# Two turns without dense products, gate steps and second product inside a mixture unit, chunk loads two units ahead

## The chip, the cores and the metric

The kernel runs on one core of one Trainium2 chip. The metric is the device time of one execution in microseconds. Three runs of the kernel before gave 909.3, 910.09 and 910.9, median 910.09 us.

## The reference

Three layers follow each other. The first is a landmark (Nyström) attention over 4 batches x 8 heads x 576 positions x 64 features; the second a dense softplus layer; the third a mixture of 8 experts of which each token uses one.

```python
k_lm = k.reshape(B, H, 32, 18, D).mean(axis=3)      # q_lm likewise
A, Bm, C = sm(q, k_lm), sm(q_lm, k_lm), sm(q_lm, k) # softmax of scaled scores
for _ in range(6):
    Z = 2 * Z - Z @ Bm @ Z                          # Newton steps to an inverse
x = A @ Z @ C @ v                                   # -> [2304, 512]
h = x @ w_in                                        # [2304, 2048]
g = np.maximum(h, 0.0) + np.log1p(np.exp(-np.abs(h)))
x = g @ w_out                                       # [2304, 512]
e_idx = argmax(x @ w_gate)                          # one of 8 experts a token
out = gate_w * sigmoid(x @ w_ogate)[e_idx] * (relu(x @ w1[e_idx]) @ w2[e_idx])
```

The weights of the dense layer arrive as 64-bit floats and are decoded on the chip.

## The kernel before

**Attention stage.** Steps named in a string (PLAN) are called one after the other: K and V load a group of four heads, T turns its keys and queries (`transposes`, line 178), M makes landmarks, A and C score, N inverts, E and F multiply out; X, W and O prepare the first chunk and the first weights. There are eight groups, g = 0 to 7. This part of the program is not written in its final order: a planner with costs for the instructions places them on the engines, so that the groups are interleaved. In a turn each of the 2 x 4 head tiles takes a PSUM bank (two of them, tag `pt`), puts a dense 128x512 product of ones into it (`warm`, line 159, whose result is overwritten), three transposes, and an eviction by ScalarE (line 187).

**Dense stage.** It stands under a manual schedule: each engine runs its instructions in the order of the code. The 2304 tokens are nine chunks c of 256; a pair p is two of the sixteen blocks of 128 columns of `w_in`. A mixture unit i (loop of line 882) is one (c, p) of the list `order`, 72 in all. It consists of

- the first product `gemm1` (line 628): 24 matmuls, twelve for each column block, from a high and a low part of tokens and weights (three products for one), into one of two PSUM banks of tag `h`;
- `softplus` (line 641): four ScalarE instructions (t, t, u, l), three of VectorE (u, d, l), then gh on ScalarE and gl on VectorE, the two parts of the result. The tiles t, u, l, d have one buffer, gh and gl three;
- the second product `gemm2` of unit i - 2 (LAG = 2): 12 matmuls into the chunk's accumulators.

The bank of `gemm1` is free again when d has read it, so unit i + 2 waits for d of unit i. The first 24 units (nj = 24) mix chunks 0, 1 and 2, with one pair of chunk 0 ahead; from unit 24 on the chunks follow one another, eight units each.

**Weights within the first 24 units.** Blocks 8 to 15 of `w_in` and 3 to 15 of `w_out` are decoded meanwhile by a generator (`weights`, line 573) of 64 weight steps: one to begin, then three for each of 21 jobs (high part on ScalarE with the start of the next job; low part on VectorE; three VectorE instructions that end the next job's decode). `softplus` calls three weight steps in each unit from 1 on: after its first ScalarE part, after gh, after gl. EXTRA = 0, 5, 8 adds one after unit 0 and three each after units 5 and 8. The jobs are sorted by the unit that needs them; blocks 12 and 13 of `w_in` are jobs 13 and 14 and are read first by unit 16 (chunk 0, pair 6), blocks 14 and 15 are jobs 17 and 18 and are read first by unit 19.

**Chunk loads.** The tokens of chunk 3 are loaded at the head of unit 23 and split after its softplus; those of chunk c + 1 are loaded and split (`load_xr`, `split_x`, lines 604 and 620) in one place, after the softplus of unit (c, 5). The loads are issued by SP's queue, which also stores the gated chunks (line 751) in the order of the code. The two load buffers carry the tag `deca` that the weight jobs use too.

**Gate steps.** When a chunk's second product is complete, `gate` (line 676) copies it out of PSUM (two ScalarE copies of line 679), and then continues in steps: transposes of one half with their ScalarE copy (line 690), logits of that half (line 695), the same for the other half, the choice of the expert on VectorE, ranks (a small matmul), and reciprocal and store. A list of waiting steps, `side`, is taken up one step after `gemm1` and one at the end of a unit; in the units 65 to 72 (`fast`) also one in the middle of each product, by `hook`. The part `early`, which finds the most frequent expert, follows the gate of chunk 7 in that list.

**Expert stage.** 23 slots of 128 gathered tokens, each with the weights of one expert, loaded and split while the slot before is multiplied. The change does not touch it.

Of the kernel before, what the change touches and what calls it, by code (L numbers as in the profile page):

```python
# [41 lines left out]
"""  # L42
NWA = 8
NWO = 3
EXTRA = 0, 5, 8
JOINT = 3
NFIRST = 2
TAIL = 0, 2, 1, 0, 1, 1, 0, 0, 1, 0, 1, 0, 0, 0, 1, 1
# [62 lines left out]
def chain(*gens):  # L111
    for g_ in gens:
        yield from g_
# [3 lines left out]
def moe_nystrom_kernel(ctx: ExitStack, tc: tile.TileContext, q, k, v, w_in, w_out, w_gate, w_ogate, w1, w2,  # L117
# [26 lines left out]
    with ExitStack() as actx:  # L144
# [14 lines left out]
        def warm(ps):  # L159

            nc.tensor.matmul(ps, dense[:, :128], dense, start=True, stop=True)  # L161
# [16 lines left out]
        def transposes(r, g):  # L178
            for nm in ("k", "q"):
                xt = a2.tile([128, 4, HALF], F32, tag=nm + "T", name=nm + "T", bufs=3)  # L180
                for h in range(4):
                    ps = pt.tile([128, 512], F32, tag="pt", name="ps_t")
                    warm(ps)
                    for c in range(3):
                        nc.tensor.transpose(ps[:, c * TP:(c + 1) * TP], r[nm][:, h, c * 128:(c + 1) * 128],  # L185
                                            ident[:TP, :TP])
                    nc.scalar.activation(xt[:, h], ps[:, :HALF], AF.Copy)
                    yield
                r[nm + "T"] = xt
# [355 lines left out]
    with ExitStack() as mctx:  # L545
# [58 lines left out]
        def load_xr(c):  # L604
            if c <= JOINT - 1:
                t = m2.tile([128, 4, CH], F32, tag="x2", name="xr", bufs=3)
                xr = [t[:, :2], t[:, 2:]]
            else:
                xr = [m2.tile([128, 2, CH], F32, tag="deca", name="xr") for _ in range(2)]
            t0 = c * CH  # L610
            while t0 < (c + 1) * CH:
                b, o = divmod(t0, S)
                n = min(S - o, (c + 1) * CH - t0)
                for j in range(2):
                    nc.sync.dma_start(xr[j][:, :, t0 - c * CH:t0 - c * CH + n],
                                      xT_d[b].rearrange("(k p) n -> p k n", p=128)[:, 2 * j:2 * j + 2, o:o + n])
                t0 += n
            return xr
# [19 lines left out]
                    hook()  # L638
            return ps

        def softplus(h, units):

            t = sp.tile([128, 2, CH], F32, tag="t", name="t")
            u = sp.tile([128, 2, CH], F32, tag="u", name="u")
            l = sp.tile([128, 2, CH], F32, tag="l", name="l")
            d = sp.tile([128, 2, CH], F32, tag="d", name="d")
            gh = m3.tile([128, 2, CH], F32R, tag="gh", name="gh")
            gl = m3.tile([128, 2, CH], F32R, tag="gl", name="gl")
            nc.scalar.activation(t, h, AF.Abs)
            nc.scalar.activation(t, t, AF.Exp, scale=-1.0)  # L650
            nc.scalar.activation(u, t, AF.Identity, bias=1.0)  # L651
            nc.scalar.activation(l, t, AF.Ln, bias=1.0)
            units(1)
            nc.vector.scalar_tensor_tensor(u, u, -1.0, t, ALU.add, ALU.subtract)  # L654
            nc.vector.scalar_tensor_tensor(d, h, 0.0, u, ALU.max, ALU.subtract)  # L655
            nc.vector.tensor_tensor(l, l, d, ALU.add)  # L656
            nc.scalar.activation(gh, l, AF.Copy)  # L657
            units(1)
            nc.vector.tensor_tensor(gl, l, gh.bitcast(F32), ALU.subtract)  # L659
            units(1)  # L660
            return gh, gl

        def gemm2(p, g, acc):
            for i in range(2):
# [188 lines left out]
        with tc.manual_schedule():  # L853
# [19 lines left out]
            def units(n):  # L873
                for _ in range(n):
                    next(work, None)
# [6 lines left out]
            for i in range(len(order) + LAG):  # L882
                fast[0] = len(order) - np_ <= i - LAG + 1 < len(order)
                if i == len(order):
                    for _ in side:
                        pass
                    win_ctx.close()
                    rw = ctx.enter_context(tc.tile_pool(name="rw", bufs=1, side="right", reuse_waits="tile"))
                    for j in range(4):
                        raw.append(rw.tile([128, 4, 512], F32, name=f"raw{j}"))  # L890
                    for _ in range(2):
                        ring[0].append([rw.tile([128, 4, 512], F32R, name=f"{n}{len(ring[0]) + 4}") for n in ("hi", "lo")])
                    wk[0] = splits(0, NBASE)
                if i < len(order):
                    c, p = order[i]
                    if i == nj - 1:
                        xr.append(load_xr(JOINT))
                    h = gemm1(p, xs[c], *HB.get(i, ()))
                    if i > nj + LAG:
                        next(side, None)  # L900
                    gs[i] = softplus(h, units if i else int)
                    if i in EXTRA:
                        units(1 if i == 0 else 3)
                    if i == 2:
                        nc.vector.tensor_copy(tri_b, cc("tri"))
                        nc.vector.tensor_copy(one_b, cc("ones"))
                        nc.vector.memset(osum[:, 0], 0.0)
                        nc.vector.tensor_copy(sgn[:, 0], cc("iota")[:1, :NE])
                        nc.vector.tensor_scalar(sgn[:, 1], cc("iota")[:1, :NE], -1.0, None, ALU.mult)
                        for nm, src in ((0, w_gate), (1, w_ogate)):  # L910
                            nc.sync.dma_start(wg[:, :, nm * NE:(nm + 1) * NE], src.rearrange("(k p) e -> p k e", p=128))
                    if i == nj - 1:
                        xs[JOINT] = split_x(xr.pop(0))
                    if p == 5 and JOINT - 1 < c < NCH - 1:
                        xs[c + 1] = split_x(load_xr(c + 1))
                if i >= len(order):
                    xt[i - len(order)] = t_x(i - len(order))
                    wunits(2)
                if i >= LAG:
                    c2, p2 = order[i - LAG]  # L920
                    if p2 == 0:
                        tags = first[c2] if c2 < JOINT else first[c2 % 2]
                        accs[c2] = [(pa if "acc" in t else pb).tile([128, 512], F32, tag=t, name=t) for t in tags]
                    gemm2(p2, gs.pop(i - LAG), accs[c2])
                    if p2 == np_ - 1:
                        ga_ = gate(c2, accs.pop(c2))
                        next(ga_)
                        side = chain(side, ga_)
                        if c2 == NCH - 2:
                            side = chain(side, early())  # L930
                if nj + LAG < i < len(order) + LAG - 1:
                    next(side, None)
            side = chain(side, route())


# [154 lines left out]
```

## Time and profile before

| | us |
|---|---|
| median of three runs | 910.09 |
| the profiled execution, as a run | 910.2 |
| its span from the first to the last instruction | 908.4 |
| around the span | 1.8 |
| TensorE busy | 859.9 (95% of the span) |
| VectorE busy | 666.5 (73%) |
| ScalarE busy | 586.9 (65%) |
| GpSimd busy | 209.5 (23%) |
| mean granted TensorE clock | 0.988 |

The attention stage takes the span up to about 136 us (its last products run till 152), the dense stage from there to about 594, the expert stage the rest. A busy share of TensorE comes from matmuls whose ends are modelled and overlap; what counts below is when each begins. A row of the timeline reads: start, duration, engine, line, operation, out<-in, shape, number merged; in brackets the idle time of the engine before it and what ended that. PE is TensorE, DVE is VectorE, ACT is ScalarE, SPq is the issuing of transfers by SyncE.

### The profile page before, as it was taken

The page shows a single profiled execution, that of the slowest core. Times are in us where ns is not written, and L with a number is a line of the kernel's source. Part 1 is how long each engine was busy: PE and PEld are TensorE (multiplying, and loading weights), DVE is VectorE, ACT ScalarE, POOL GpSimd, SP SyncE. Part 2 cuts the span into 40 slices and gives each one's busy share as a digit, 9 for nine tenths or more (in the row PEclk, how much of TensorE's full clock was granted, in tenths as well). Part 3 has the DMA queues.
Part 4 walks back from the last instruction along what each step waited for, and adds up shares of the span by engine and source line. Part 5 has one row for each costly group of instructions (what it writes and reads, how often), then busy time and mean ns, then how long its engine had stood idle before and what let it go on. Part 6 is the DMA issues. An engine that isn't in the chain of part 4 may idle for free.

```text
span 908.4 us, 15419 instructions
## 1 busy us (share of the span) xinstructions
PE 859.9 (95%) x5826; PEld 718.9 (79%) x5826; DVE 666.5 (73%) x1121; ACT 586.9 (65%) x958; POOL 209.5 (23%) x109
## 2 busy tenths in 40 slices
PE   6998987989998999998999998989999999999996
PEld 3665655888997999998899997877888888888885
DVE  0856697999984465556556463668799999999994
ACT  2554565767774655555455554465888888888883
POOL 0001131000000000000000000034666667666662
PEclk9999999999999999999999999999999999999998
DMA  9856555333300000101011000141118369521600
GB/s 222 196 140 183 158 189 166 95 116 97 113 24 24 1 25 1 47 24 47 1 48 47 1 25 1 47 186 59 36 40 292 148 222 366 185 105 35 232 26 33
DMA packets 49516, 90.92 MB, mean 100 GB/s; under 512 B 5471, under 2 KB 32095, under 8 KB 47392
## 3 DMA queue, kind: packets, MB, share of 16 engines
q1 hardware_dynamic: 41408, 74.43, 26.6%
q0 software_dynamic: 3680, 10.78, 3.7%
q10 hardware_dynamic: 4352, 4.72, 1.5%
q8 instruction: 46, 0.75, 0.4%
q14 instruction: 30, 0.25, 0.1%
HBM read 134.46 MB, written 15.48 MB: 165 GB/s over the span
## 4 chain that ended last, share of the span: by engine, by line
PE 68%; DVE 14%; DMA 6%; ACT 6%; issue 4%; POOL 0%; SPq 0%; DVEq 0%; POOLq 0%; ACTq 0%
PE ps_h L635 19%; PE acc L670 15%; PE ps_g L960 10%; PE ps_y L985 9%; DMA raw<-in_moe_w 3%; DVE lo L479 2%; DVE dect L101 2%; PE ps_hT L974 2%; ACT hi L477 2%; PE ps_lg L695 2%; DVE deca L102 1%; PE ps_t L185 1%; PE ps_t L161 1%; DVE l L656 1%; DVE d L655 1%
## 5 line engine op out<-in xcount | busy, mean ns | idle before, releaser
L479 DVE TENSOR_TENSOR lo<-raw,hi 128x1024 fp32r<-128x1024 f32 x129 | 226.3, 1781 | 11.4 <-ACT hi L477 11.1
L477 ACT ACTIVATE hi<-raw 128x1024 fp32r<-128x1024 f32 x176 | 176.9, 1063 | 8.5 <-DMA raw<-in_moe_w 8.1
L635 PE MATMUL ps_h<-xh,whi 128*128 128x256 f32 x512 | 148.1, 289 | 7.7 <-DVE d L655 4.8
L635 PE MATMUL ps_h<-xl,whi 128*128 128x256 f32 x512 | 146.3, 286 | 0.4 <-DVE xl L108 0.4
L635 PE MATMUL ps_h<-xh,wlo 128*128 128x256 f32 x512 | 146.2, 286 | 0.0
L486 POOL DMA_INDIRECT xg<-x_d,gidx x23 | 37.0, 1610 | 444.1 <-ACT t L650 433.1
L479 POOL TENSOR_TENSOR lo<-raw,hi 128x1024 fp32r<-128x1024 f32 x47 | 116.7, 2485 | 35.8 <-ACT hi L477 35.6
L657 ACT ACTIVATE gh<-l 128x512 fp32r<-128x512 f32 x72 | 45.5, 632 | 116.0 <-DVE l L656 116.0
L654 DVE SCALAR_TENSOR_TENSOR u<-u,t 128x512 f32<-128x512 f32 x72 | 49.6, 688 | 83.5 <-ACT u L651 83.4
L635 PEld LDWEIGHTS ps_h<-xh,whi 128*128 128x128 f32 x512 | 99.2, 194 | 13.6 <-DVE d L655 6.1
L670 PE MATMUL acc<-woh,gh 128*128 128x512 f32 x256 | 103.1, 403 | 1.6 <-ACT gh L657 1.6
L670 PE MATMUL acc<-wol,gh 128*128 128x512 f32 x256 | 101.0, 394 | 0.0
L635 PEld LDWEIGHTS ps_h<-xl,whi 128*128 128x128 f32 x512 | 99.2, 194 | 2.2 <-DVE xl L108 0.6
L670 PE MATMUL acc<-woh,gl 128*128 128x512 f32 x256 | 100.8, 394 | 0.0
L635 PEld LDWEIGHTS ps_h<-xh,wlo 128*128 128x128 f32 x512 | 99.4, 194 | 0.0
L659 DVE TENSOR_TENSOR gl<-l,gh 128x512 fp32r<-128x512 f32 x72 | 49.9, 693 | 38.8 <-ACT gh L657 37.0
L985 PE MATMUL ps_y<-hi,woh 128*128 128x512 f32 x184 | 76.7, 417 | 0.2 <-ACT woh L977 0.2
L985 PE MATMUL ps_y<-hi,wol 128*128 128x512 f32 x184 | 73.3, 398 | 1.4 <-DVE wol L978 1.3
L960 PE MATMUL ps_g<-hi,x0l 128*128 128x512 f32 x184 | 73.9, 402 | 0.3
L985 PE MATMUL ps_y<-lo,woh 128*128 128x512 f32 x184 | 72.7, 395 | 0.0
L960 PE MATMUL ps_g<-hi,x0h 128*128 128x512 f32 x184 | 72.1, 392 | 0.0
L960 PE MATMUL ps_g<-lo,x0h 128*128 128x512 f32 x184 | 71.9, 391 | 0.0
(246 smaller groups left out, 1756.6 us busy)
## 6 DMA issues: line engine op xcount, KB each, us to landing
raw<-in_moe_w SPq DMA_DIRECT2D x88, 1024.0 KB
raw<-in_moe_w_in SPq DMA_DIRECT2D x16, 512.0 KB
raw<-in_moe_w_out SPq DMA_DIRECT2D x16, 512.0 KB
x_d<-x SPq DMA_DIRECT2D x9, 514.0 KB
k<-in_k SPq DMA_DIRECT2D x8, 576.0 KB
q<-in_q SPq DMA_DIRECT2D x8, 576.0 KB
v<-in_v SPq DMA_DIRECT2D x8, 576.0 KB
xT_d<-xo ACTq DMA_DIRECT2D x16, 288.0 KB
```

The lines of the kernel that those rows point to most:

```text
L101: nc.vector.scalar_tensor_tensor(t, hi32, -0x80000000, t, ALU.bitwise_and, ALU.bitwise_or)
L477: nc.scalar.activation(w[0][:, us], raw[i][:, us], AF.Copy)
L479: eng.tensor_tensor(w[1][:, us], raw[i][:, us], w[0][:, us].bitcast(F32), ALU.subtract)
L486: nc.gpsimd.indirect_dma_start(out=xg, out_offset=None, in_=src, in_offset=bass.IndirectOffsetOnAxis(ap=gidx[:, s:s + 1], axis=0))
L635: nc.tensor.matmul(ps[:, i], a[:, kk], b_[:, kk], start=n == 0, stop=n == 11)
L654: nc.vector.scalar_tensor_tensor(u, u, -1.0, t, ALU.add, ALU.subtract)
L657: nc.scalar.activation(gh, l, AF.Copy)
L659: nc.vector.tensor_tensor(gl, l, gh.bitcast(F32), ALU.subtract)
L670: nc.tensor.matmul(acc[tt], a[:, i, ts_], b_[f], start=f == 0 and n == 0, stop=f == NFF - 1 and n == 2)
L695: nc.tensor.matmul(pl[:, :2 * NE], xt[tt][:, kk], wg[:, kk], start=kk == 0, stop=kk == 3)
L960: nc.tensor.matmul(ps, a[:, kk], b_[:, kk], start=n == 0, stop=n == 11)
L985: nc.tensor.matmul(y, a[:, kk], b_[:, kk], start=half == 0 and n == 0, stop=half == 1 and n == 11)
```

## The change

- The turns of groups 3 and 4 lose their dense products, eight each.
- `softplus` becomes a generator of four parts. Its first two parts (the ScalarE four, the VectorE three) stay behind `gemm1`; then come `gemm2` of unit i - 2 with the gate steps at its middle and end and the copies that begin a gate; then gh, and then gl. In ScalarE's and VectorE's queues the end-of-unit gate step now stands ahead of gh and gl. TensorE's order is not altered.
- EXTRA = 15, 15, 15: after unit 15 three weight steps more; none after 0, 5 and 8 (unit 0 has its one step by the new rule).
- The load of chunk 3 stands at the end of unit 21 and its split at the end of unit 22; the load of chunk c + 1 at the end of unit (c, 3), its split at the end of unit (c, 5).

```diff
--- before.py
+++ after.py
@@ -42,7 +42,7 @@
 """
 NWA = 8
 NWO = 3
-EXTRA = 0, 5, 8
+EXTRA = 15, 15, 15
 JOINT = 3
 NFIRST = 2
 TAIL = 0, 2, 1, 0, 1, 1, 0, 0, 1, 0, 1, 0, 0, 0, 1, 1
@@ -180,7 +180,8 @@
                 xt = a2.tile([128, 4, HALF], F32, tag=nm + "T", name=nm + "T", bufs=3)
                 for h in range(4):
                     ps = pt.tile([128, 512], F32, tag="pt", name="ps_t")
-                    warm(ps)
+                    if g not in (3, 4):
+                        warm(ps)
                     for c in range(3):
                         nc.tensor.transpose(ps[:, c * TP:(c + 1) * TP], r[nm][:, h, c * 128:(c + 1) * 128],
                                             ident[:TP, :TP])
@@ -638,27 +639,27 @@
                     hook()
             return ps
 
-        def softplus(h, units):
+        def softplus(h):
 
             t = sp.tile([128, 2, CH], F32, tag="t", name="t")
             u = sp.tile([128, 2, CH], F32, tag="u", name="u")
             l = sp.tile([128, 2, CH], F32, tag="l", name="l")
             d = sp.tile([128, 2, CH], F32, tag="d", name="d")
-            gh = m3.tile([128, 2, CH], F32R, tag="gh", name="gh")
-            gl = m3.tile([128, 2, CH], F32R, tag="gl", name="gl")
             nc.scalar.activation(t, h, AF.Abs)
             nc.scalar.activation(t, t, AF.Exp, scale=-1.0)
             nc.scalar.activation(u, t, AF.Identity, bias=1.0)
             nc.scalar.activation(l, t, AF.Ln, bias=1.0)
-            units(1)
+            yield
             nc.vector.scalar_tensor_tensor(u, u, -1.0, t, ALU.add, ALU.subtract)
             nc.vector.scalar_tensor_tensor(d, h, 0.0, u, ALU.max, ALU.subtract)
             nc.vector.tensor_tensor(l, l, d, ALU.add)
+            yield
+            gh = m3.tile([128, 2, CH], F32R, tag="gh", name="gh")
+            gl = m3.tile([128, 2, CH], F32R, tag="gl", name="gl")
             nc.scalar.activation(gh, l, AF.Copy)
-            units(1)
+            yield
             nc.vector.tensor_tensor(gl, l, gh.bitcast(F32), ALU.subtract)
-            units(1)
-            return gh, gl
+            yield gh, gl
 
         def gemm2(p, g, acc):
             for i in range(2):
@@ -893,26 +894,13 @@
                     wk[0] = splits(0, NBASE)
                 if i < len(order):
                     c, p = order[i]
-                    if i == nj - 1:
-                        xr.append(load_xr(JOINT))
-                    h = gemm1(p, xs[c], *HB.get(i, ()))
+                    g = softplus(gemm1(p, xs[c], *HB.get(i, ())))
                     if i > nj + LAG:
                         next(side, None)
-                    gs[i] = softplus(h, units if i else int)
-                    if i in EXTRA:
-                        units(1 if i == 0 else 3)
-                    if i == 2:
-                        nc.vector.tensor_copy(tri_b, cc("tri"))
-                        nc.vector.tensor_copy(one_b, cc("ones"))
-                        nc.vector.memset(osum[:, 0], 0.0)
-                        nc.vector.tensor_copy(sgn[:, 0], cc("iota")[:1, :NE])
-                        nc.vector.tensor_scalar(sgn[:, 1], cc("iota")[:1, :NE], -1.0, None, ALU.mult)
-                        for nm, src in ((0, w_gate), (1, w_ogate)):
-                            nc.sync.dma_start(wg[:, :, nm * NE:(nm + 1) * NE], src.rearrange("(k p) e -> p k e", p=128))
-                    if i == nj - 1:
-                        xs[JOINT] = split_x(xr.pop(0))
-                    if p == 5 and JOINT - 1 < c < NCH - 1:
-                        xs[c + 1] = split_x(load_xr(c + 1))
+                    next(g)
+                    if 0 < i < nj:
+                        units(1)
+                    next(g)
                 if i >= len(order):
                     xt[i - len(order)] = t_x(i - len(order))
                     wunits(2)
@@ -930,6 +918,25 @@
                             side = chain(side, early())
                 if nj + LAG < i < len(order) + LAG - 1:
                     next(side, None)
+                if i < len(order):
+                    next(g)
+                    if 0 < i < nj:
+                        units(1)
+                    gs[i] = next(g)
+                    if i < nj:
+                        units(1 + EXTRA.count(i))
+                    if i == 2:
+                        nc.vector.tensor_copy(tri_b, cc("tri"))
+                        nc.vector.tensor_copy(one_b, cc("ones"))
+                        nc.vector.memset(osum[:, 0], 0.0)
+                        nc.vector.tensor_copy(sgn[:, 0], cc("iota")[:1, :NE])
+                        nc.vector.tensor_scalar(sgn[:, 1], cc("iota")[:1, :NE], -1.0, None, ALU.mult)
+                        for nm, src in ((0, w_gate), (1, w_ogate)):
+                            nc.sync.dma_start(wg[:, :, nm * NE:(nm + 1) * NE], src.rearrange("(k p) e -> p k e", p=128))
+                    if i == nj - 3 or p == 3 and JOINT - 1 < c < NCH - 1:
+                        xr.append(load_xr(max(c + 1, JOINT)))
+                    if i == nj - 2 or p == 5 and JOINT - 1 < c < NCH - 1:
+                        xs[max(c + 1, JOINT)] = split_x(xr.pop(0))
             side = chain(side, route())
```

## Rows read from the trace of the kernel before

**Rows 1.** The page's chain that ended last, shares of the span by engine

```profile
PE 68%; DVE 14%; DMA 6%; ACT 6%; issue 4%; POOL 0%; SPq 0%; DVEq 0%; POOLq 0%; ACTq 0%
```

**Rows 2.** Chain that ended last, in order of time: start, us, what

```profile
13.45 0.48 PE ps_t L185 x3
...
287.53 4.34 PE ps_h L635 x23
...
300.44 2.87 PE ps_h L635 x24
303.31 2.75 PE acc L670 x12
...
431.07 4.31 PE acc L670 x12
...
561.67 4.47 PE ps_h L635 x24
```

**Rows 3.** Waits of PE, 160 to 600: waiter, releaser, us in total, times, longest

```profile
PE ps_h L635 <- DVE d L655: 4.8, 3, 2.4
...
PE ps_h L635 <- ACT xh L107: 2.8, 1, 2.8
PE ps_n L767 <- DVE cd L736: 1.8, 1, 1.8
PE ps_tr L689 <- ACT x L679: 1.8, 2, 1.4
```

**Rows 4.** Timeline, ACT at the turn to chunk 3

```profile
286.06 1.13 ACT L107 ACTIVATE xh<-xr 128x512 fp32r<-128x512 f32 x2
```

**Rows 5.** Windows: length, busy us (count) by engine, clock, DMA share, GB/s

```profile
288.00:292.00 4.00, 4.00 (x23) 4.00 (x22) 0.08 (x1) 0.03 (x1) 0.00 (x0) 0.59 0.50 131
...
560.00:564.00 4.00, 3.39 (x21) 3.39 (x22) 2.06 (x9) 0.55 (x2) 0.00 (x0) 0.73 0.00 0
```

**Rows 6.** Timeline, the load and split of chunk 6

```profile
422.91 0.36 SPq L751 DMA_DIRECT2D x_d<-x  x1
...
423.36 2.44 SPq L615 DMA_DIRECT2D xr<-xT_d  x4
...
428.32 1.15 ACT L107 ACTIVATE xh<-xr 128x512 fp32r<-128x512 f32 x2 [1.60 <-DMA xr<-xT_d]
...
430.01 1.07 PE L695 MATMUL ps_lg<-wg,x2t 128*128 128x16 f32 x8 [2.51 <-ACT x2t L690]
```

**Rows 7.** Timeline, gate of chunk 7

```profile
559.98 0.58 ACT L690 ACTIVATE x2t<-ps_tr 128x512 f32<-128x512 f32 x1
...
560.61 1.06 PE L695 MATMUL ps_lg<-wg,x2t 128*128 128x16 f32 x8 [1.36 <-ACT x2t L690]
```

**Rows 8.** Timeline, first 24 units: PE's waits for d, VectorE's unit

```profile
177.34 0.39 PE L635 MATMUL ps_h<-xh,whi 128*128 128x256 f32 x1 [0.24 <-DVE d L655]
...
210.57 0.39 PE L635 MATMUL ps_h<-xh,whi 128*128 128x256 f32 x1 [2.17 <-DVE d L655]
...
242.06 0.69 DVE L655 SCALAR_TENSOR_TENSOR d<-ps_h,u 128x512 f32<-128x512 f32 x1
...
243.47 0.69 DVE L599 TENSOR_TENSOR wol<-deca,woh 128x512 fp32r<-128x512 f32 x1
...
247.44 0.69 DVE L655 SCALAR_TENSOR_TENSOR d<-ps_h,u 128x512 f32<-128x512 f32 x1
```

**Rows 9.** Timeline, the turn of group 3 and the first piece of group 5's

```profile
46.54 0.39 PE L161 MATMUL ps_t<-dense 128*128 128x512 bf16 x1
46.77 0.41 PE L185 MATMUL ps_t<-cst,k 96*128 96x96 f32 x3
...
47.21 0.90 ACT L187 ACTIVATE kT<-ps_t 128x288 f32<-128x288 f32 x2 [0.23 <-PE ps_t L185]
...
48.34 0.90 ACT L187 ACTIVATE kT<-ps_t 128x288 f32<-128x288 f32 x2 [0.23 <-PE ps_t L185]
...
73.52 0.39 PE L161 MATMUL ps_t<-dense 128*128 128x512 bf16 x1
```

## The prediction

> **What bounds the kernel.** I read the page's chain of work first: TensorE holds 68% of it [rows 1], so a microsecond counts where TensorE stands still or runs slowly. The chain in order of time then shows the dense stage at its best: a first product in 2.87 us and a second in 2.75, one after the other, 5.62 us a unit [rows 2]. TensorE can't be shortened there except by its interruptions, and the table of TensorE's waits lists them, each a handful of places rather than a pattern [rows 3]. The chain has a second sign of an interruption: pieces that take 4.3 to 4.5 us where 2.75 to 2.87 are usual [rows 2]. They follow the waits, and the granted clock falls in them (0.59 in the mean of 288 to 292, 0.73 in 560 to 564 [rows 5]; 1.00 is the 2.4 GHz level, so part of such a stretch runs at 1.2). So a wait of 1.4 to 2.8 us costs up to 1.6 us more behind it, though not each does.
>
> **Loads in front, chunk 3.** Now the split stands behind the softplus of unit 23, and ScalarE gets to xh at 286.06 [rows 4], when TensorE has waited for most of 2.8 us [rows 3]; it runs freely only from 287.53, 0.9 us behind xh's first half (286.06 + about 0.57), because xl comes later. Then 23 matmuls take 4.34 us instead of 2.75. Together 2.8 + 0.9 + 1.6 = 5.3. After the change the split ends unit 22, one unit (5.62 us) earlier. xh and xl then take some 2.5 us behind gl of unit 22, and unit 24 begins about 4 us behind that point, so nothing is late: **-5.2**. The split pushes the softplus of unit 23 back by its 1.13 us of ScalarE; the two banks give d far more room than that. The load needs the buffers that the last weight job gives back in unit 20, and is issued in unit 21, so it has landed when unit 22 ends.
>
> **Loads in front, chunk 6.** SP stores chunk 3's gate result at 422.91 and only then issues the four loads, at 423.36; ScalarE reaches the split and stands 1.60 us for the data; the gate's copy is queued behind that, and TensorE waits 2.51 us for it before its logits [rows 6]. The second product behind it takes 4.31 instead of 2.75 us [rows 2]. At pair 3 the load is ahead of that store in SP's queue, two units earlier: -2.5 - 1.6 = **-4.1**. The other turns show no wait and gain nothing. What is queued behind the earlier loads on SP are only stores that nobody waits for in that stretch.
>
> **Gate steps ahead of gh.** ScalarE idles between l's first part and gh, because VectorE's three instructions come between. A copy or exponential that fits there is free. Before, the copies that begin a gate and the copy of the second turn stood behind gh; in chunk 7's gate TensorE waited 1.4 us for the first, 1.36 for the second (ScalarE starts it at 559.98, TensorE runs on at 560.61) and 1.8 for VectorE to free the bank of the ranks [rows 3, 7]; another 0.4 of the same kind lies at chunk 4's gate (1.8 in two waits, the longest 1.4 [rows 3]). The first product after the second wait took 4.47 instead of 2.87 [rows 2]. With gh behind them, both copies are done before TensorE asks. The ranks' bank depends on VectorE's work behind l of unit 67, which starts earlier by gl and its wait (about 1.2 us), so some 0.6 of 1.8 remain; and `early`, whose VectorE work is not shortened, now comes last: I expect 0.7 of a new wait at its second matmul. Sum: 1.4 + 1.4 + 1.8 + 1.6 - 0.6 - 0.7 + 0.4 = 5.3, **-5.3**. gl itself comes later by the gate's VectorE work (at most some 2.5 us in a unit), but unit i + 2 uses it, 11 us later. Moving `gemm2` into the unit alters no order on TensorE: nothing.
>
> **EXTRA.** The two long waits for d are the price of the extra steps after units 5 and 8: 2.4 and 2.17 [rows 3, 8]. They go, -4.6. But the weights come later. Unit 16 reads block 13, whose low part is weight step 45. Before, steps 1 + 3 x 12 + 6 = 43 are done after unit 12, and 45 falls into unit 13. Now 1 + 3 x 14 = 43 are done after unit 14, and 45 is the middle step of unit 15: its VectorE instruction stands behind d and l of unit 15, and ends 1.4 us after d (243.47 + 0.69 against 242.06 + 0.69 [rows 8]). How early is d? VectorE needs 5.38 us a unit (242.06 to 247.44) and TensorE 5.62, so d gains 0.24 a unit from where it was just in time, the 0.24 us wait at 177.34 for unit 6 [rows 8]: by unit 15's d eleven units, 2.6 us ahead of unit 17's start. The low part is then ready 1.2 us ahead of unit 17. Unit 16 wants it in its second half, 1.6 us after its own start, so 4.0 us ahead of unit 17. TensorE waits about 2.8 there, inside a first product. Unit 19 meets the same with block 15 (step 57, the middle of unit 18), because the three extra steps after unit 15 take VectorE back by about what the wait gave: some 2.4. Gains 4.6, new waits about 5: **+0.3**. Bounds: -4.6 if no weight is late, +3.5 if both waits are followed by slow pieces like the 1.6 above.
>
> **The turns.** Sixteen dense products go, each 0.23 us of TensorE (46.54 to 46.77). In group 3's turn two evictions of together 0.90 us come every 1.13 us (47.21, 48.34), and the bank's round trip contains the dense product [rows 9]; without it the period falls to the 0.90 of ScalarE: four times 0.23, 0.9 us. In group 4's turn other groups' products lie between, TensorE is the bound and up to 8 x 0.23 = 1.8 is to be had. This stage's order comes from a planner, though, which will place its instructions anew, and behind 78 us the chain goes through VectorE and transfers. Bounds: -2.7 with all of it, and 4 us lost where a new order or the clock is bad (at the low level three transposes take 0.48 us, as at 13.45 [rows 2]). I take **-1.8**, nearest to the counted rows, since TensorE, which is what is relieved, carries the chain here.
>
> **Sum.** -5.2 - 4.1 - 5.3 + 0.3 - 1.8 = -16.1 us, against the profiled execution's 910.2 (span 908.4 and 1.8 around it; the median of the runs is 910.09, no different): 894.1, **894**. The expert stage starts from the last first product and moves along as a whole.
>
> A rule speaks against one part. The dense products keep TensorE occupied where transposes of 96 columns don't. The Trainium skill, page "TensorE: Matmul & The Clock Gate", Part 1 (the HAM clock gate), says that the throttled state is the default and that activity releases it; by that rule the turns could run at 1.2 GHz, and the sum would be that of rival (a) below, 900 in place of 894. The trace has both answers: the clock fell after waits of 2.8 and 1.4 us, and no slow piece follows the waits of 2.4 and 2.17.
>
> **Rivals.** (a) *The clock drops at the two bare turns and recovers soon.* For it: the slow pieces above; against: other groups' dense products remain between the two turns. The products of one turn and its surroundings at half speed, some 4 us, and the 1.8 not gained: 900. Chance 0.17, with it a plan of the attention stage that is worse by as much. (b) *The weights are not late,* because the gaps leave VectorE further ahead than I count, or the planner gains more: 889.5. Chance 0.11. (c) *A gate step in front of gh holds the softplus up*: where ScalarE waits for TensorE's transposes or VectorE for logits, gh, gl and then the next l slip, and d with them; 1 us for each of eight chunks takes half the gain: 902. Against it: TensorE's step ends about when l is ready. Chance 0.08. (d) *Slower*: the clock drops at group 3's turn and stays at 1.2 GHz until group 5's turn, where dense products stand again: from 46.54 to 73.52 [rows 9], 27 us, nearly all of it TensorE's. If TensorE's work there, at least 22 us, takes twice as long, that is +22 against the remaining -14.3: 918. It decides from a low stretch of about 15 us on. Chance 0.05. (e) *No change to be seen*: the dense stage is under a manual order, so that the loads and steps do move; only if the planned stage gives back just what the rest gains. Chance 0.03. The forecast itself: 0.56.
>
> **Range and chances.** From (b) with some room, 887, to (c), 902; left out are (d), (e) and the far ends. A measurement can tell 0.2%, about 1.8 us, from no change. Faster: 0.92 (forecast, a, b, c); the same 0.03; slower 0.05.
>
> **What would show it.** In the changed profile the wait of ps_h for xh is gone, and so is the 2.5 us wait of the logits behind the split of chunk 6; both 4.3 us pieces read 2.75 to 2.87. In place of two waits of ps_h for d two of ps_h for the low part of `w_in` (line 599) stand in units 16 and 19, about 2.5 us each. From unit 66 to 69 the waits for x2t and x are gone, those of the small matmuls are under 1 us. The period of evictions in group 3's turn is 0.90. The prediction is wrong if the clock in 46 to 75 is under 0.9, if ScalarE's gh waits longer than l needs, or if the first product of unit 24 still waits.

## The result, and the profile after

Four executions of the changed kernel took 894.88 to 898.59 us, median 897.45; four of the kernel before, beside them, 909.69. The ratio is 0.9861 (95% interval 0.9835 to 0.9886): faster by 12.2 us where 16.1 were forecast, inside the range. The profiled execution took 898.08 with a span of 896.3, 12.1 less than before. So 4 us are missing, and the table of the units' first matmuls says where. Each line is the start of a unit's first product in the profile of the kernel before and of the changed kernel.

```text
unit                        before    after    shift   change since the line above
 3 (attention has ended)    160.08   163.73    +3.65   +3.65
23 (last of the mixed ones) 278.11   282.12    +4.01   +0.36
25 (chunk 3 has begun)      294.65   293.36    -1.29   -5.30
47 (behind chunk 6's split) 435.71   430.05    -5.66   -4.37
66 (chunk 7's gate)         550.10   543.69    -6.41   -0.75
70 (expert stage follows)   582.75   570.86   -11.89   -5.48
```

All of the gain lies in the dense stage, 15.5 us of it from unit 3 on; the attention stage, where 1.8 were to be gained, ends 3.65 later. The chain of the page, shares of the span by engine, gives TensorE 70% now [rows 1]:

```profile
PE 70%; DVE 16%; issue 4%; ACT 4%; DMA 4%; POOL 0%; SPq 0%; DVEq 0%; POOLq 0%; ACTq 0%
```

The waits of TensorE from 160 to 600 in the changed kernel (waiter, releaser, us in total, times, longest):

```profile
PE ps_h L636 <- DVE wlo L600: 3.0, 2, 1.6
PE ps_rk L727 <- DVE oh L721: 2.3, 1, 2.3
PE ps_i L792 <- DVE erhs L787: 0.5, 1, 0.5
PE ps_n L768 <- DVE cd L737: 0.4, 1, 0.4
PE ps_h L636 <- ACT whi L597: 0.3, 1, 0.3
```

Against [rows 3], the waits for d, xh and x are gone. Two for the low part have come; ps_n is down from 1.8 to 0.4, and ps_i is new at 0.5. The 2.3 of ps_rk is not new: before, the same wait ends at 611.50, outside the window. Timelines of the changed kernel, at the places of [rows 4] and [rows 6 to 9]:

```profile
46.47 1.88 ACT L188 ACTIVATE kT<-ps_t 128x288 f32<-128x288 f32 x4
48.41 1.88 ACT L188 ACTIVATE qT<-ps_t 128x288 f32<-128x288 f32 x4
...
240.37 0.39 PE L636 MATMUL ps_h<-x0h,wlo 128*128 128x256 f32 x1 [1.32 <-DVE wlo L600]
...
259.67 0.39 PE L636 MATMUL ps_h<-x0h,wlo 128*128 128x256 f32 x1 [1.63 <-DVE wlo L600]
...
284.45 1.14 ACT L107 ACTIVATE xh<-xr 128x512 fp32r<-128x512 f32 x2
...
423.37 0.60 ACT L691 ACTIVATE x2t<-ps_tr 128x512 f32<-128x512 f32 x1 [0.40 <-PE ps_tr L690]
...
425.34 1.13 ACT L107 ACTIVATE xh<-xr 128x512 fp32r<-128x512 f32 x2
...
426.04 0.96 PE L696 MATMUL ps_lg<-wg,x2t 128*128 128x16 f32 x8
```

The split of chunk 3 starts at 284.45 for a unit that begins at 287.74. The split of chunk 6 finds its data, and the gate's copy (423.37) runs ahead of it, so the logits carry no bracket. In group 3's turn the second four evictions start 1.94 behind the first four (46.47, 48.41), 0.97 a pair, where 0.90 was forecast and 1.13 stood before. Windows of the changed kernel (length, busy us by engine, granted clock, DMA share, GB/s):

```profile
48.00:52.00 4.00, 3.39 (x40) 1.84 (x42) 0.00 (x0) 2.38 (x6) 0.00 (x0) 1.00 0.40 106
...
88.00:92.00 4.00, 0.63 (x16) 0.09 (x16) 0.25 (x1) 0.94 (x2) 0.00 (x0) 1.00 0.72 164
92.00:96.00 4.00, 3.40 (x27) 2.77 (x28) 4.00 (x9) 1.94 (x5) 0.42 (x1) 0.62 0.01 2
...
160.00:164.00 4.00, 4.00 (x13) 3.06 (x13) 3.79 (x8) 3.33 (x6) 0.00 (x0) 0.66 0.22 42
...
260.00:264.00 4.00, 4.00 (x17) 3.47 (x16) 2.35 (x5) 2.11 (x4) 0.00 (x0) 0.57 0.02 4
...
288.00:292.00 4.00, 4.00 (x30) 3.75 (x29) 2.20 (x4) 1.72 (x3) 0.00 (x0) 1.00 0.30 80
```

The two windows of the loss, in the kernel before:

```profile
88.00:92.00 4.00, 2.65 (x42) 1.63 (x42) 2.22 (x7) 1.87 (x4) 0.00 (x0) 1.00 0.70 194
92.00:96.00 4.00, 3.72 (x35) 2.89 (x34) 4.00 (x9) 2.66 (x6) 1.66 (x1) 1.00 0.47 145
```

288 to 292 is back at 1.00 [rows 5]. The loss shows in 88 to 96: TensorE, busy for 2.65 us of 88 to 92 before, is busy for 0.63, then runs at a mean clock of 0.62. Unit 0 begins 2.3 later than before; another 1.3 come in unit 2, where a wait of 1.8 us for gh (1.6 before) is followed by a clock of 0.66 in 160 to 164 (1.00 before). The bare turns themselves ran at 1.00 here.

### The profile page after: what moved, and what is told of

Its sections match the earlier page's. It is cut to its first block, busy times and chain, and to the rows that moved or that the text cites. A ratio compares the mean times of both kernels' runs of the same rounds, so it can differ in the third digit from the quotient of the medians.

```text
span 896.3 us, 15388 instructions
## 1 busy us (share of the span) xinstructions
PE 856.1 (96%) x5810; PEld 716.8 (80%) x5810; DVE 667.1 (74%) x1121; ACT 587.1 (66%) x958; POOL 210.2 (23%) x109
## 4 chain that ended last, share of the span: by engine, by line
PE 70%; DVE 16%; issue 4%; ACT 4%; DMA 4%; POOL 0%; SPq 0%; DVEq 0%; POOLq 0%; ACTq 0%
PE ps_h L636 17%; PE acc L671 16%; PE ps_g L967 12%; PE ps_y L992 11%; DVE dect L101 2%; DVE deca L102 2%; PE ps_hT L981 2%; PE ps_t L186 2%; PE ps_lg L696 2%; DVE lo L480 2%; DVE l L655 2%; DVE d L654 1%; DVE u L653 1%; ACT gh L659 1%; DVE dect L100 1%
```

## The experiments

Each kernel was timed in at least five executions, beside the kernel before on the same chip.

**All dense products back** (changed kernel, line 183: `warm(ps)` without the condition).

> The changed kernel with the sixteen dense products back in the turns of groups 3 and 4. In the changed profile unit 3 of the dense stage begins 3.65 us later than before (163.73 against 160.08), where I had forecast 1.8 earlier. Theory R (taking the dense products away is the cause, by a later second transfer of weights and TensorE standing idle behind it): this kernel begins unit 3 at about 160.1, and takes 897.5 - 3.6 = 893.9 us. Rival V (those 3.65 are a variation of the transfer and of the clock from one execution to the next): unit 3 begins anywhere between 160 and 164, and the median is that of the changed kernel, 897.5, within 1. Rival F (the removal gains its 1.8 us as forecast, and something else in the change costs the rest): 899.3.

894.33 us (892.99 to 895.50); ratio 0.9820 (0.9806 to 0.9833), clear of the changed kernel's interval (0.9835 to 0.9886). Unit 3 began at 159.20. The removal costs time.

**Bare turns alone** (kernel before; `if g not in (3, 4): warm(ps)`).

> The kernel before with only the dense products of groups 3 and 4 taken out. Theory R: unit 3 begins at about 163.7 and the time is 909.7 + 3.6 = 913.3 us. Rival V: 909.7 within 1. Rival F, the forecast's own term: 909.7 - 1.8 = 907.9.

913.33 us; ratio 1.0024 (1.0003 to 1.0044). Slower, if by less than Theory R's 3.6; the forecast's -1.8 (ratio 0.998) is excluded. Its profiled execution, at 922.41, lay far above that median; windows of it:

```profile
48.00:52.00 4.00, 3.88 (x31) 2.28 (x34) 1.00 (x2) 2.88 (x7) 0.00 (x0) 0.81 0.60 147
52.00:56.00 4.00, 3.47 (x39) 1.94 (x31) 0.00 (x0) 0.77 (x2) 0.00 (x0) 0.50 0.17 37
...
68.00:72.00 4.00, 4.00 (x36) 1.96 (x34) 1.85 (x8) 1.79 (x3) 0.00 (x0) 0.63 0.27 93
```

This is the mechanism of rival (d) at half its price: 1.2 GHz from group 3's turn until about 70, and unit 3 11.4 us late where (d) counted 22. Two of the twelve executions lie that high (920.76 and 922.41); neither profile of the changed kernel has any of it.

**Loads alone** (kernel before; the two statements with `load_xr` and `split_x` taken to the end of the unit, as in the change).

> The kernel before with only the chunk loads in front (chunk 3 at the end of unit 21 with its split at the end of unit 22, the others at the end of pair 3 with the split at the end of pair 5). The forecast's terms, 5.2 for chunk 3 and 4.1 for chunk 6: 909.7 - 9.3 = 900.4 us; the two turns of the changed profile measure 5.3 + 4.4 = 9.7, so 900.0. Rival: the gates in their old place behind gh meet the split in another way, so that chunk 6 gains nothing and only 5 are left, 904.5.

900.14 us, ratio 0.9878 (0.9862 to 0.9894). Chunk 3's turn gained 5.30, chunk 6's 4.33 (from the units' starts). Unit 67 is 1.5 shorter as well: both waits of chunk 7's gate still stand in unit 66 (1.37 and 1.36), but no slow piece follows the second one in this profile.

**Extra steps alone** (kernel before; `EXTRA = 0, 15`).

> The kernel before with EXTRA = 0, 15: three weight steps more after unit 15 in place of three after unit 5 and three after unit 8. The forecast's term is +0.3, 910.0 us: the two waits of ps_h for d (2.4 and 2.17) gone, a wait for the low part of w_in in unit 16 and one in unit 19, 1.6 to 2.8 us each. Rival by the forecast's bounds: 905.1 if no weight is late, 913.2 if both waits are followed by slow pieces.

910.49 us, ratio 0.9990 (0.9976 to 1.0003). From unit 3 to unit 23 the shift changes from -0.32 to -0.35: gain and price cancel.

**Gate steps alone** (changed kernel with the dense products, loads and extra steps of before).

> The kernel before with only the new order in a unit: second product and gate steps ahead of gh and gl; loads, weight steps (EXTRA) and dense products as before. The forecast's term is -5.3; in the changed profile the units 50, 58 and 66 to 69 gain 0.6, 0.15 and 5.5 = 6.2. So 911.1 - 6.2 = 904.9 us, 905.8 by the forecast. Rival (c) of the forecast, gate steps that hold the softplus up by 1 us for each of eight chunks: 904.9 + 8 = 913. Rival: the gain at units 66 to 69 belongs to the earlier loads and not to the order, then 911.

904.39 us, ratio 0.9932 (0.9913 to 0.9952). The sum is the expected one, but not by the expected terms. Units 66 to 70 gained 3.7 and unit 47 4.37, with the loads in their old place: the gate's copy no longer stands behind the split there. Chunk 6's 4.3 us can be had by either part, and only once. With the late loads, 2.4 were lost again: ScalarE stood 4.80 and 4.68 us at the splits of the next two chunks (xh at 481.40 and 530.61) for data, and TensorE waited for d in front of units 56 and 64, which the kernels with early loads don't show.

**One bare turn at a time** (changed kernel; `if g != 3`, then `if g != 4`).

> The changed kernel with the dense products of group 4's turn back, so that only group 3's turn is bare. The kernel with all of them took 894.3 us, the changed kernel 897.5 (median of its own call). Both bare kernels issue the load of v 0.67 us behind the second load of raw (1.03 before and with all dense products) and get raw's data 5.9 us after its issue instead of 3.65; TensorE then stands still in 88 to 92. Theory D (a bare turn brings the load of v forward, and that makes raw late; every kernel with the short distance loses the 3 to 4 us): whichever of the two turns shows the distance of 0.67 also shows raw 5.9 us after its issue and takes 897 to 898, and the other takes 894 to 895. Rival P (it is the placing of the instructions as such): 5.9 us also with a distance of 1.03. Rival C (what costs is the clock at group 3's turn): some runs of this kernel are at 905 or above, as two of twelve were in the kernel before with bare turns (920.8 and 922.4, clock 0.50 from 52 to 68), and none with only group 4's turn bare.

> The changed kernel with the dense products of group 3's turn back, so that only group 4's turn is bare. As for the other turn: Theory D, 897 to 898 us if the load of v comes 0.67 us behind that of raw, 894 to 895 if 1.03. Rival C, the clock falls at group 3's turn alone: then no run of this kernel is far above its median. The forecast's count for this turn, up to 1.8 us gained: 892.5.

Group 3's turn bare: 898.65 us (895.61 to 900.75, six executions), 895.61 and 895.97 at mean clocks of 0.990 and 0.991, the rest at 0.984 or 0.985. TensorE's timeline in the profiled execution (900.05):

```profile
46.70 1.94 PE L186 MATMUL ps_t<-cst,k 96*128 96x96 f32 x12
48.63 2.17 PE L186 MATMUL ps_t<-cst,q 96*128 96x96 f32 x12
50.73 0.64 PE L198 MATMUL ps_l<-q,lmc 96*32 96x256 f32 x2
```

The products ps_l take 0.64 here and 0.39 to 0.41 in the changed kernel's profile: the clock fell within the turn, and the windows give 0.50 from 52 to 60. Unit 3 began at 164.30; the second raw landed 3.93 us behind its issue. No execution reached the 905 that Rival C asked for: the low stretch is 10 us here, and 20 in the kernel with bare turns alone.

Group 4's turn bare: 898.51 us (898.20 to 899.40). No fall at the turn; SP, ScalarE and TensorE in 82 to 94:

```profile
82.15 3.91 SPq L391 DMA_DIRECT2D raw<-in_moe_w_in  x2
86.36 0.33 SPq L174 DMA_DIRECT2D v<-in_v  x1
...
91.70 1.22 ACT L98 ACTIVATE deca<-raw 128x512 f32<-128x512 f32 x2 [4.16 <-DMA raw<-in_moe_w_in]
...
93.24 1.12 PE L206 MATMUL ps_lm<-lmc,l 128*64 128x64 f32 x16 [4.05 <-ACT l L202]
```

The first row merges both issues of raw; the second begins 0.37 before its end, at 82.15 + 3.91 - 0.37 = 85.69, and lands at 91.67. ScalarE stands 4.16 us for it, l's eviction is queued behind, and TensorE stands 4.05 us. With all dense products (first experiment) the same rows read:

```profile
81.40 3.68 SPq L390 DMA_DIRECT2D raw<-in_moe_w_in  x2
85.75 0.33 SPq L174 DMA_DIRECT2D v<-in_v  x1
...
88.31 1.22 ACT L98 ACTIVATE deca<-raw 128x512 f32<-128x512 f32 x2 [1.37 <-DMA raw<-in_moe_w_in]
...
89.84 0.69 PE L205 MATMUL ps_lm<-lmc,l 128*64 128x64 f32 x16 [1.25 <-ACT l L201]
```

So the two turns cost in two ways: Rival C's clock at group 3's, in some executions, and the late raw at group 4's. Both profiles of the changed kernel have the late raw and not the fall. Distance and lateness went together as Theory D says, which proves nothing of cause; hence the next two.

**Load of v later** (group 4's turn bare; ahead of the load of group 6's v, `nc.gpsimd.memset(t[:, 0], 0.0)`).

> The kernel with only group 4's turn bare (898.5 us), in which GpSimd writes zeros into a part of the buffer of v ahead of the load of group 6's v (96x384, overwritten by the load), so that this load is issued some 0.5 us later. The order of the instructions on TensorE, VectorE, ScalarE and SP is the same. Theory D (the transfer of v, issued 0.67 us behind the second load of raw, makes raw late): with the load of v 1.0 us or more behind, raw lands 3.6 to 3.9 us after its issue in place of 5.98, TensorE's stand in 88 to 92 goes, unit 3 begins 3 to 4.5 us earlier than 163.73, and the time is 894 to 895, with a part of the forecast's gain at group 4's turn 893.5. Rival P (the order of the instructions makes the stand, however v is loaded): raw 5.9 us after its issue or TensorE still at 88 to 92, 898.5.

897.28 us (895.12 to 897.58), ratio 0.9853 (0.9832 to 0.9873); by time not to be told from 0.9864 (0.9845 to 0.9884) without the memset. The trace decides:

```profile
82.41 3.96 SPq L391 DMA_DIRECT2D raw<-in_moe_w_in  x2
87.13 0.33 SPq L174 DMA_DIRECT2D v<-in_v  x1
...
91.26 1.22 ACT L98 ACTIVATE deca<-raw 128x512 f32<-128x512 f32 x2 [3.42 <-DMA raw<-in_moe_w_in]
```

v is 1.13 behind raw, and raw still lands 5.23 us after its issue. Theory D falls but for a share of 0.75 (5.98 - 5.23). The trace's records of the single parts show why: a landing has sixteen parts, and fifteen came 3.02 to 3.60 us after the issue, as with dense products; the sixteenth came alone at 5.23. The Trainium skill, page "DMA: Bandwidth & Descriptors", section "Why a DMA increments its semaphore by 16 and not by 1", says that a transfer runs on up to sixteen engines that finish independently; by that the consumer waits for the slowest, and the trace agrees. What held one part up? Beside raw's queue (q1) the view of transfers has one record at that moment, a piece of code of 16 KB (queue q8; here 88 to 89 of the kernel with group 4's turn bare):

```profile
q8 instruction: 1, 0.02, 6.0%
```

Its start in each profile, and the landings, in us behind the second raw's issue:

```text
kernel                                code piece   15 parts by   last part
eight with group 4's dense products   2.77-3.09     3.47-3.77    3.57-3.93
group 4's turn bare (four profiles)   2.00-2.57     4.04-4.49    5.83-6.41
 and v later                          2.25          3.60         5.23
```

The packets show where the piece falls. Raw has 512 packets of 1 KB, of which the first starts 1.0 us behind the issue. With group 4's dense products 429 to 501 of them have started when the piece does, and by 3.4 us all have (in one profile all but one); with the turn bare 153 to 367 have, and 10 to 18 are left that start one by one from 3.4 until 4.2 to 5.0 us. So the bare turn brings the piece from the end of raw's packets into the middle of them. The fifteen other parts go with v: they are there by 4.04 to 4.49 where v is 0.66 or 0.67 behind raw, and by 3.47 to 3.77 where it is 1.03 or more. The piece seems to belong to TensorE's program: the kernel before has 46 of them for 11652 recorded matmuls and weight loads, and this one comes behind 2047 with all dense products, 2033 with group 4's turn bare, 2012 and 2014 with both. Which instruction calls it is not pinned down by that.

**Code piece earlier** (group 4's turn bare; sixteen more dense products in the first head tile of group 0).

> The kernel with only group 4's turn bare (898.5 us), with sixteen more dense products at the very beginning (1.5 to 9.9 us, where TensorE waits for the first transfers), so that everything that TensorE's instructions reach by their number (the loading of its own code in pieces of 16 KB) comes 32 instructions earlier in its program; the order of the other engines, and of TensorE behind them, is the same. In the three kernels with group 4's turn bare and in the one with the later load of v, such a piece is loaded from 2.0 to 2.6 us behind the issue of the second raw, and one of raw's sixteen parts lands last, 5.2 to 6.4 us behind the issue; in the eight kernels with that turn's dense products it is loaded from 2.8 to 3.1 us on, and the sixteenth part lands with the others, at 3.6 to 3.9. Theory L (that piece of code occupies one of the sixteen DMA engines when raw's part stands in it): now the piece is loaded from about 0.4 to 1.4 us behind the issue, its 0.9 to 1.4 us are over before the bulk of raw's packets, raw's last part lands 3.6 to 4.5 us behind the issue, TensorE's stand in 88 to 92 shrinks by 1.5 to 2.2, and the time is about 896.5. Rival: raw's last part lands 5.2 us or more behind its issue wherever the code is loaded, and the time stays at 898.5 but for what the beginning gains or loses.

896.18 us (894.68 to 899.79), ratio 0.9837 (0.9814 to 0.9860). The piece was loaded 0.79 behind raw's issue, ahead of all its packets; seven of these started after 3.4, the last at 3.74, and raw's last part landed at 4.56:

```profile
80.64 3.98 SPq L391 DMA_DIRECT2D raw<-in_moe_w_in  x2
84.91 0.33 SPq L174 DMA_DIRECT2D v<-in_v  x1
...
88.84 1.22 ACT L98 ACTIVATE deca<-raw 128x512 f32<-128x512 f32 x2 [2.74 <-DMA raw<-in_moe_w_in]
...
90.38 0.69 PE L206 MATMUL ps_lm<-lmc,l 128*64 128x64 f32 x16 [2.64 <-ACT l L202]
```

The stand shrinks from 4.05 to 2.64, the clock behind it is 1.00 (0.53 with group 4's turn bare), and unit 3 begins at 158.90 where it was 163.73; some 1.4 of that is the earlier beginning, since raw itself is issued at 84.25. That beginning has a cause of its own: with the added products TensorE's clock is on record at 1.00 from 7.36 us, in the other profiles from 13.6 to 16.4, and group 0's turn ends at 14.01 instead of 15.53. The piece came behind 2027 recorded instructions, with 32 more in front, so it goes by TensorE's count here and not by its place in the work. v is 0.66 behind raw, as in the kernel that lands it at 5.98, which is one more case against Theory D. Theory L holds in the trace, if at the edge of what it said (4.56 for 3.6 to 4.5, 1.4 of stand for 1.5 to 2.2). The times don't decide: by the rival 898.5 - 1.4 = 897.1 would be left, within the interval; the other executions scatter, and no profile shows why. That piece and sixteenth part meet on one engine of the sixteen is argued, not shown: the records don't name the engine.

**The changed kernel again.**

> The changed kernel as it is, on the chip of the two runs above. 897.5 us by its first four runs, 3.1 above the kernel with all dense products (894.3, another call); if both bare turns act here, one always (stand behind the late raw) and one in a part of the executions (clock at group 3's turn), its runs scatter more than those of the other kernels, from 895 upwards.

898.08 us (897.68 to 898.90), ratio 0.9866 (0.9847 to 0.9886). The scatter that I expected did not come. The piece of code at 2.12, the last part at 6.41, in this profile too.

**Low part on GpSimd** (all dense products; `nc.gpsimd.tensor_tensor(lo, ...)`, `finish` one step earlier, six extra steps).

> The changed kernel with all dense products, and in the first 24 units the low part of a decoded weight taken on GpSimd (1.27 to 1.5 us for 128x512 in the attention stage) instead of VectorE (0.69), the decode's end one step earlier, between l and gl where VectorE waits for gh, and EXTRA = 9, 9, 9, 13, 13, 13. Worked out from the durations, VectorE then needs about 4.6 us a unit in place of 5.38, d runs ahead of TensorE by 1 us a unit, the waits for d and for the low part both go, and unit 24 begins 4.3 us earlier than with the weight steps of the changed kernel: 894.3 - 4.5 = 890 us. Rival: GpSimd and VectorE slow each other down when both work on 128x512 tiles, the waits for d come back: 894 or above.

896.74 us, ratio 0.9839 (0.9820 to 0.9859): the rival. The group of l on VectorE from 160 to 275 (busy us, mean ns, idle before), first here, then with all dense products and the low part on VectorE:

```profile
L654 DVE TENSOR_TENSOR l<-l,d 128x512 f32<-128x512 f32 x20 | 27.6, 1379 | 2.1
...
L654 DVE TENSOR_TENSOR l<-l,d 128x512 f32<-128x512 f32 x21 | 14.5, 693 | 2.2
```

One of them, and GpSimd's product beside it, in the timeline:

```profile
230.65 1.48 DVE L654 TENSOR_TENSOR l<-l,d 128x512 f32<-128x512 f32 x1
...
230.27 1.31 POOL L599 TENSOR_TENSOR wlo<-deca,whi 128x512 fp32r<-128x512 f32 x1 [4.28 <-ACT whi L596]
```

l has a mean of 1379 ns where it had 693: it starts under GpSimd's product and ends 0.55 behind that product's end. The 0.69 that VectorE was to save is spent there, and two waits for d (3.7 us) come back.

**Six extra steps** (all dense products; `EXTRA = 14, 14, 14, 16, 16, 16`).

> The changed kernel with all dense products and EXTRA = 14, 14, 14, 16, 16, 16 (one job's three weight steps more, three after unit 14 and three after unit 16, in place of three after unit 15). With them blocks 13 and 15 are ready one unit earlier: theory, the two waits for the low part (1.58 in unit 16 and 1.6 in unit 19 in the changed profile) go, the six steps cost a wait for d in unit 16 and one in unit 18 of together about 3, and unit 24 begins 1.8 us earlier than with 15, 15, 15: 894.3 - 1.8 = 892.5. Rival: the waits for d are as long as the waits for the weights were and are followed by slow pieces: 894 to 896.

892.23 us (891.68 to 894.07), ratio 0.9805 (0.9785 to 0.9826): the lowest median of the study, though its interval overlaps that of the kernel with 15, 15, 15 (0.9806 to 0.9833). TensorE's waits from 150 to 300:

```profile
PE ps_h L635 <- ACT deca L98: 1.8, 1, 1.8
...
PE ps_h L635 <- DVE wlo L599: 0.2, 1, 0.2
PE ps_h L635 <- DVE d L653: 0.2, 1, 0.2
```

From unit 0 to unit 24 it gains 1.86 on the kernel with 15, 15, 15; the long waits for the low part are down to 0.2. The price is one wait of 1.8 in front of unit 19 (put down to deca, but d of unit 17 ended within 0.1 us of it).

## Why the prediction was right, and where it failed

The time came inside the range because the dense stage gave 15.5 us by the units' starts in the changed kernel, and 15.9 in the kernel with all dense products, where 14.3 were forecast, and because the term that failed lost less than the rivals allowed for.

**Chunk 3, -5.2: right** (5.30 with the change, 5.30 with the loads alone).

**Chunk 6, -4.1: right in size** (4.37), though counted for one cause: the loads alone take the wait away, and so does the order of the gate steps alone. The forecast's "at pair 3 the load is ahead of that store" is true and is not needed.

**Gate steps, -5.3: 6.2 measured** (0.75 and 5.48, from the units' starts). ps_n was left with 0.4 instead of 0.6; the new wait forecast for `early` came, 0.5 instead of 0.7. The 0.4 that the forecast put at chunk 4's gate is the wait in unit 50, at chunk 5's, and gave 0.6. Of the 5.48, 1.5 are the slow piece behind the second wait, which was absent with the loads alone too, so not all of the sum is owed to the order. Rival (c) did not appear.

**EXTRA, +0.3: right as a sum, with some luck** (0.36; 0.0 by itself). The two waits came in units 16 and 19 as named, 1.3 and 1.6 (with whi's 0.3 ahead of the second) instead of 2.8 and 2.4. The second was followed by a clock of 0.57 in 260 to 264, which the forecast had only in its bounds. In three other profiles with these weight steps (the changed kernel again, group 3's turn bare, the code piece earlier) the same stretch from unit 3 to unit 23 cost 1.5, each with that slow piece; in four without it, 0.0.

**The turns, -1.8: the step that failed.** "I take -1.8 [...] since TensorE, which is what is relieved, carries the chain here" did not come true. The turns themselves became shorter, but nothing of it was left 8 us later. The profiles start group 3's turn at 44.3 to 47.0, for reasons that lie in front of it (45.97 after, 46.54 before), so I count from there; the two kernels whose clock fell in the turn are left out:

```text
                                   ps_l behind  group 4's  next    second     unit
                                   the turn     turn ends  ps_l    raw        3
both turns dense (seven profiles)  4.51-4.52    13.6       20.07   39.0-39.2  113.5-113.9
both bare (two profiles)           3.87         12.4       20.08   39.2       116.8-117.8
group 4's turn bare                4.52         13.1       20.73   39.8       117.9
 and v later                       4.52         13.1       20.74   39.9       116.5
 and code piece earlier            4.52         13.1       20.73   39.9       114.6
```

Group 3's turn gave 0.64 of the counted 0.9, both together 1.2 by the end of group 4's. At the next ps_l the lead is gone. TensorE's rows, before and after:

```profile
51.05 0.41 PE L197 MATMUL ps_l<-q,lmc 96*32 96x256 f32 x2
...
66.60 0.39 PE L197 MATMUL ps_l<-q,lmc 96*32 96x256 f32 x2
```

```profile
45.97 1.94 PE L186 MATMUL ps_t<-cst,k 96*128 96x96 f32 x12
...
49.84 0.41 PE L198 MATMUL ps_l<-q,lmc 96*32 96x256 f32 x2
...
60.41 1.24 PE L379 MATMUL ps_x<-at,wbd 64*128 64x288 f32 x8 [0.24 <-DVE wbd L369]
...
64.15 0.71 PE L267 MATMUL ps_r<-btbd 128*128 128x128 f32 x4
...
66.05 0.39 PE L198 MATMUL ps_l<-q,lmc 96*32 96x256 f32 x2
```

TensorE now waits for ScalarE and VectorE (0.20 and 0.24), and the planner has placed anew what follows: the inversion's first product ps_r stands ahead of these ps_l in every kernel with group 4's turn bare, and behind them in the others. So raw is issued no earlier, as counted from the turn. Then the piece of TensorE's code falls among raw's packets; the last part came 2.3 us later than before, and a stand with a slow piece followed: 3.1 to 4.1 us at unit 3. With the piece moved, most of that is gone (114.6), which bears out the cause as far as one profile can. The prediction's own bound "behind 78 us the chain goes through VectorE and transfers", 4 us lost, held the result; the value was taken at the wrong end. With the products kept the whole gain is 911.06 - 894.33 = 16.7.

**Rivals.** (a) had the likely place and its addition, "a plan of the attention stage that is worse by as much", came nearest to what happened. Its clock is half shown: after a bare turn 3 the clock falls in some executions; at group 4's turn it did in no profile. (d)'s long fall was seen once, in the kernel with bare turns alone. The rule named with (a), that activity releases the throttled state (the Trainium skill, page "TensorE: Matmul & The Clock Gate", Part 1), bears on that: in the execution that fell, the engine had done nothing in the turn but 96-column transposes, one tile every 0.48 us. The rows don't settle it, since the same transposes at the same pace ran at 1.00 in both profiles of the changed kernel.

## What to carry to other kernels

Time taken from an engine is worth something only up to the next place where it waits for another engine or a transfer; compare the lead behind that place, not the time removed, and where a planner orders the program, look whether the order is still the same. When two parts of a change remove the same wait, test each alone before adding their terms. An interruption has to be priced with the slow clock behind it, and that price varies between executions of one program: of the changed kernel's two profiles one has a slow piece of 1.3 us behind unit 2, the other none.

## What was not expected of the hardware

Code is loaded while the program runs: 46 pieces of 16 KB in the queue q8 (of the kind "instruction") in the changed kernel's 896 us, 0.9 to 1.4 us each around the place studied. Where one fell among the packets of a 512 KB transfer, one sixteenth of that transfer landed 1.4 to 2.1 us behind the rest. Eight products fewer on TensorE, with the order that the planner made of it, were enough to move it there.

A VectorE instruction with both inputs in SBUF took 1.38 us in the mean in place of 0.69 where GpSimd worked on a product of 1.31 us; d of the same units, which reads PSUM, ran under such products too and stayed at 0.69. The Trainium skill, page "SBUF — State Buffer", section "Terms", says that VectorE and GpSimd share one port pair as an exclusive lock and the loser blocks; the trace agrees, in the l that ended 0.55 behind the product and in the d that did not wait.
